# Transposing x and u by crossbar DMA transfers in place of TensorE, in a convolution followed by a token-and-channel mixing layer

## The chip, the cores and the metric

The kernel runs on one core of a Trainium2 chip. The metric is device time in microseconds (us) of one execution, median of several runs; "the granted clock" is the share of full speed that the throttle gave TensorE. PE is TensorE (matmul), PEld its weight load, DVE VectorE, ACT ScalarE, POOL GpSimd, SP SyncE; SPq, ACTq and POOLq are these engines' sequencers, which here mostly issue DMA transfers.

## The reference

```python
# x: (8, 4224, 192); batch B = 8, tokens S = 4224, channels D = 192
x = causal_conv7(x, softmax(weight))           # 8 heads, 7 taps
theta = x @ w_theta                            # 192 x 192
zr, zi = x * cos(theta), x * sin(theta)
y = einsum('ts,bsd->btd', w_tok_r, zr) + einsum('ts,bsd->btd', w_tok_i, zi)   # 4224 x 4224 twice
u = x + y
out = u + relu(u @ w_ch)                       # 192 x 192
```

The two token products are nearly all of the arithmetic. In both kernels the two channel products take their left operand with channels on the partitions. x and u are made with tokens on the partitions, so both are transposed; how that is done is what this study changes.

## The kernel before

Tokens are cut into 33 chunks of 128. A chunk is built once: convolution by TensorE (`conv`), transposition (`transpose`), `theta`, cosine and sine, products with x, and sums. It then stays in SBUF as `z` for 17 steps of token matmuls. There are 58 steps. Each handles one pair of row blocks of the token matrices and up to 11 live chunks, in 7 runs (a step of 11 chunks has 7 x 11 x 2 = 154 matmuls of 128x384). 11 chunks are built in the opening, before the steps flow freely; the other 22 are built in two later stages, about two a step. In the last 17 steps (the final ones) each step also finishes its rows: `cast` u to fp16, transpose it, `output`. The last five, with fewer live chunks, are called late.

Work is emitted in program order with positions: a task at position p of a step comes before the matmul at p/7 of it. In the traces each of PE, DVE, ACT and POOL works in that order; a scheduler places the transfers of SP's one queue.

```python
    def transposed(u, by_dve=False):
        tp = banks("tp", F16)                    # one of two PSUM buffers, shared with pc and v
        for k in range(6):
            pe(nc.tensor.transpose(
                tp[:, 0, k * P : (k + 1) * P], u[:, k * P : (k + 1) * P], ident
            ))
        uT = wk.tile([P, 6, P], F16, name="uT", tag="uT")
        evacuate(uT[:, :, :].rearrange("p k s -> p (k s)"), tp[:, 0, 0 : 6 * P], by_dve)
        return uT
# ... cut ...
        def conv(self, j):
            # ... cut: 8 matmuls into pc, evacuated by ACT into self.x ...
            if j == 1:
                for a in range(NQ):
                    t0 = token(self.k, a)
                    nc.sync.dma_start(
                        out=xs[t0 : t0 + Q, :], in_=self.x[a * Q : (a + 1) * Q, :]
                    )

        def transpose(self, g):
            self.xT[g] = transposed(
                self.x[:, g * GC : (g + 1) * GC], 0 < self.k < 3 or (self.k, g) == (0, 1)
            )

        def theta(self, g):
            v = channel_mix(self.xT[g], wth).rearrange(
                "p k (b h e) -> p k b h e", b=2, h=2
            )
            # ... cut: two ACT sines of v into z ...
# ... cut ...
        def turn_u(self, i, g):
            self.uT[i, g] = transposed(self.ub[i, g])
# ... cut: outputs(), times in us after the step's end ...
                    at = 0.7 + 12 * i
                    every, turn, mix = 3.6, 2.9, 4.7
# ... cut: step_events(t), positions of a new chunk's ten tasks (conv x2, transpose x2, theta x2, products, sums);
# the kernel after has eleven, with the store of x after the transposes ...
                pos = [0, .5, 1.3, 1.6, 2.1, 2.5, 3.1, 3.15, 3.4, 3.6]
# ... cut: the opening, one turn per chunk; old is the chunk before ...
        if ch:
            ch.conv(0)
        between(2)
        if old:
            old.theta(0)
        between(1)
        if ch:
            ch.conv(1)
        # ... cut ...
        if old:
            old.theta(1)
        # ... cut ...
        if ch:
            ch.transpose(0)
        if old:
            old.product(Z11)
        between(1)
        if ch:
            ch.transpose(1)
```

## Time and profile before

| | before |
|---|---|
| time | 1468.77 us (3 runs, 1468.66 to 1469.96) |
| PE busy | 98% of the span |
| token matmuls | 81% of the chain that ended last |
| granted clock | 0.996 |
| DMA share | 0.6 in quiet stages, 1.0 or more in the opening and the chunk stages |

From the page of the kernel before: busy us of each engine with its share of the span; the chain that ended last; groups of instructions (line, engine, operation, tiles, count, busy us, mean ns of one, idle time of the engine just before); issues of transfers, with median us to landing.

```profile
PE 1434.6 (98%) x10095; PEld 905.6 (62%) x10095; DVE 1001.0 (68%) x1050; ACT 360.7 (25%) x461; POOL 430.3 (29%) x659
...
PE 91%; DVE 3%; ACT 3%; DMA 1%; issue 1%; POOL 0%; DVEq 0%; ACTq 0%; POOLq 0%
PE y L408 81%; PE v L138 6%; PE tp L153 3%; ACT z L233 2%; PE pc L196 2%; DMA st<-in_moe_w_tok_i_dram 1%; DVE pv L373 1%; DVE z L244 1%; DVE z L238 0%; DVE wt L308 0%; DVE pv L437 0%; ACT uT L148 0%; DVE wt L320 0%; ACT pv L371 0%; ACT z L148 0%
...
L408 PE MATMUL y<-z,wt 128*128 128x384 f16 x7656 | 1295.3, 326 | 7.7 <-DVE pv L373 6.8
...
L148 ACT ACTIVATE uT<-tp 128x768 f16<-128x768 f16 x127 | 102.3, 813 | 296.8 <-PE tp L153 294.9
...
L138 PE MATMUL v<-wch,uT 128*128 128x192 f16 x528 | 56.9, 254 | 3.5 <-DVE pv L437 1.9
L138 PE MATMUL v<-wth,uT 128*128 128x192 f16 x528 | 54.3, 246 | 3.1 <-ACT z L233 3.0
...
L153 PE MATMUL tp<-ident,z 128*128 128x128 f16 x396 | 33.4, 222 | 8.8 <-ACT z L233 8.3
...
pv<-part SPq DMA_DIRECT2D x79, 768.0 KB, 5.4
out_dram<-pv SPq DMA_DIRECT2D x66, 384.0 KB, 4.5
st<-in_moe_w_tok_r_dram POOLq DMA_DIRECT2D x136, 176.0 KB, 5.8
...
xs<-z SPq DMA_DIRECT2D x132, 96.0 KB, 4.5
```

PE almost never waits: 7.7 us before the token matmuls in the whole span, 3.1 us before the theta products. The theta products wait for ACT's sines (z, L233: 3.0 of the 3.1 us), which read the PSUM buffer that the product takes, never for a transfer.

Windows of the kernel before: stretch, its length, busy us of each engine with instruction counts, granted clock, mean DMA share of the 16 engines (over 1 where packets overlap), GB/s.

```profile
50.00:100.00 50.00, 43.39 (x396) 28.27 (x394) 42.38 (x61) 42.72 (x58) 15.77 (x28) 1.00 0.98 221
500.00:600.00 100.00, 100.00 (x767) 63.64 (x765) 76.25 (x89) 38.02 (x48) 27.44 (x49) 1.00 1.04 248
1300.00:1400.00 100.00, 99.52 (x739) 66.05 (x738) 71.78 (x70) 25.51 (x33) 36.08 (x43) 1.00 0.91 212
```

In the opening (50 to 100 us) PE is 87% busy, and in the chunk stage from 500 us it is full while the DMA engines already show a share of 1.04. What a group of six transposes costs is read from starts in the timeline (start, duration, engine, line, instructions), since ends of matmuls are modelled:

```profile
1083.34 0.50 PE L153 MATMUL tp<-ident,ub 128*128 128x128 f16 x6
1083.68 1.79 PE L408 MATMUL y<-z,wt 128*128 128x384 f16 x10
1085.30 0.82 PE L138 MATMUL v<-wch,uT 128*128 128x192 f16 x8
```

The group holds PE for 1083.68 - 1083.34 = 0.34 us.

### The profile page before, as it was taken

The page shows a single profiled execution, that of the slowest core. Times are in us where ns is not written, and L with a number is a line of the kernel's source. Part 1 is how long each engine was busy: PE and PEld are TensorE (multiplying, and loading weights), DVE is VectorE, ACT ScalarE, POOL GpSimd, SP SyncE. Part 2 cuts the span into 40 slices and gives each one's busy share as a digit, 9 for nine tenths or more (in the row PEclk, how much of TensorE's full clock was granted, in tenths as well). Part 3 has the DMA queues.
Part 4 walks back from the last instruction along what each step waited for, and adds up shares of the span by engine and source line. Part 5 has one row for each costly group of instructions (what it writes and reads, how often), then busy time and mean ns, then how long its engine had stood idle before and what let it go on. Part 6 is the DMA issues. An engine that isn't in the chain of part 4 may idle for free.

```text
span 1469.8 us, 24434 instructions
## 1 busy us (share of the span) xinstructions
PE 1434.6 (98%) x10095; PEld 905.6 (62%) x10095; DVE 1001.0 (68%) x1050; ACT 360.7 (25%) x461; POOL 430.3 (29%) x659
## 2 busy tenths in 40 slices
PE   7789999999999999999999999999999999999997
PEld 4556666666666666666666666666666666666665
DVE  6884655454548687766656658769777787778575
ACT  6861101111134353000000015254122222121224
POOL 7422211111223322211113232332233333453220
PEclk9999999999999999999999999999999999999998
DMA  9976756574699999887879989999778777999873
GB/s 172 227 155 145 144 104 144 96 151 89 149 232 212 232 224 263 193 198 167 209 162 239 200 194 229 201 232 256 128 191 197 173 182 185 224 237 217 196 201 108
DMA packets 234975, 274.16 MB, mean 187 GB/s; under 512 B 69104, under 2 KB 202608, under 8 KB 234864
## 3 DMA queue, kind: packets, MB, share of 16 engines
q0 software_dynamic: 163616, 95.30, 49.0%
q1 hardware_dynamic: 71248, 177.30, 34.1%
q8 instruction: 79, 1.29, 0.3%
q14 instruction: 32, 0.26, 0.1%
HBM read 245.49 MB, written 111.28 MB: 243 GB/s over the span
## 4 chain that ended last, share of the span: by engine, by line
PE 91%; DVE 3%; ACT 3%; DMA 1%; issue 1%; POOL 0%; DVEq 0%; ACTq 0%; POOLq 0%
PE y L408 81%; PE v L138 6%; PE tp L153 3%; ACT z L233 2%; PE pc L196 2%; DMA st<-in_moe_w_tok_i_dram 1%; DVE pv L373 1%; DVE z L244 1%; DVE z L238 0%; DVE wt L308 0%; DVE pv L437 0%; ACT uT L148 0%; DVE wt L320 0%; ACT pv L371 0%; ACT z L148 0%
## 5 line engine op out<-in xcount | busy, mean ns | idle before, releaser
L408 PE MATMUL y<-z,wt 128*128 128x384 f16 x7656 | 1295.3, 326 | 7.7 <-DVE pv L373 6.8
L408 PEld LDWEIGHTS <-wt 128*128 128x128 f16 x7656 | 737.5, 98 | 475.0 <-issue 10.4
L373 DVE TENSOR_TENSOR pv<-y,pv 128x768 f32<-128x768 f32 x324 | 308.5, 953 | 374.2 <-PE y L408 348.6
L308 DVE STREAM_TRANSPOSE wt<-st 128x1408 f16<-128x1408 f16 (+7 forms) x224 | 326.4, 1463 | 7.7 <-DMA st<-in_moe_w_tok_i_dram 7.0
L295 POOL DMA_DIRECT2D st<-in_moe_w_tok_i_dram x232 | 132.7, 581 | 497.7 <-DVE wt L308 473.7
L295 POOL DMA_DIRECT2D st<-in_moe_w_tok_r_dram x232 | 132.7, 581 | 459.0 <-DVE wt L308 443.7
L320 DVE TENSOR_TENSOR wt<-wt 128x1408 f16<-128x1408 f16 (+7 forms) x216 | 204.1, 945 | 9.5 <-PE y L408 6.6
L148 ACT ACTIVATE uT<-tp 128x768 f16<-128x768 f16 x127 | 102.3, 813 | 296.8 <-PE tp L153 294.9
L148 ACT ACTIVATE z<-pc 128x768 f16<-128x768 f32 x65 | 52.9, 814 | 386.5 <-PE pc L196 386.5
L371 ACT ACTIVATE pv<-y 128x768 f32<-128x768 f32 x66 | 53.7, 813 | 281.5 <-PE y L408 281.5
L138 PEld LDWEIGHTS <-uT 128*128 128x128 f16 x1056 | 93.0, 99 | 25.9 <-issue 9.9
L437 DVE SCALAR_TENSOR_TENSOR pv<-v,pv 128x768 f32<-128x768 f32 x66 | 62.7, 949 | 46.8 <-PE v L138 45.5
L183 POOL DMA_DIRECT2D xw<-in_x_dram x132 | 76.5, 591 | 35.8 <-issue 10.1
L427 ACT ACTIVATE ub<-pv 128x768 f16<-128x768 f32 x66 | 54.8, 837 | 90.6 <-DVE pv L373 89.5
L244 DVE TENSOR_TENSOR z<-z 128x768 f16<-128x768 f16 x132 | 73.4, 556 | 3.8
L233 ACT ACTIVATE z<-v,half_pi 128x768 f16<-128x768 f32 x66 | 59.6, 903 | 40.0 <-PE v L138 39.8
L238 DVE TENSOR_TENSOR z<-z 128x1536 f16<-128x1536 f16 x66 | 60.4, 950 | 10.8 <-ACT z L233 10.8
L355 POOL TENSOR_TENSOR pv<-pv,xr 128x1536 f32<-128x1536 f32 x20 | 62.9, 3144 | 7.9 <-issue 4.5
L138 PE MATMUL v<-wch,uT 128*128 128x192 f16 x528 | 56.9, 254 | 3.5 <-DVE pv L437 1.9
L138 PE MATMUL v<-wth,uT 128*128 128x192 f16 x528 | 54.3, 246 | 3.1 <-ACT z L233 3.0
L233 ACT ACTIVATE z<-v 128x768 f16<-128x768 f32 x66 | 53.2, 805 | 0.0
L153 PE MATMUL tp<-ident,z 128*128 128x128 f16 x396 | 33.4, 222 | 8.8 <-ACT z L233 8.3
(43 smaller groups left out, 201.5 us busy)
## 6 DMA issues: line engine op xcount, KB each, us to landing
part<-pv SPq DMA_DIRECT2D x79, 768.0 KB, 4.3
pv<-part SPq DMA_DIRECT2D x79, 768.0 KB, 5.4
out_dram<-pv SPq DMA_DIRECT2D x66, 384.0 KB, 4.5
st<-in_moe_w_tok_r_dram POOLq DMA_DIRECT2D x136, 176.0 KB, 5.8
st<-in_moe_w_tok_i_dram POOLq DMA_DIRECT2D x136, 176.0 KB, 4.9
xs<-z SPq DMA_DIRECT2D x132, 96.0 KB, 4.5
xw<-in_x_dram POOLq DMA_DIRECT2D x121, 96.0 KB, 5.9
part<-xs POOLq DMA_DIRECT2D x26, 384.0 KB, 7.4
```

Of the source, the lines that this page charges most:

```text
L138: pe(nc.tensor.matmul(v[:, k, b * D : (b + 1) * D], lhsT=tT[:, 3 * k + b + i, :], rhs=w[:, 2 * b + i, :], start=(i == 0), stop=(i == 1),))
L148: act(nc.scalar.activation(out=out, in_=in_, func=AT.Copy))
L153: pe(nc.tensor.transpose(tp[:, 0, k * P : (k + 1) * P], u[:, k * P : (k + 1) * P], ident))
L183: nc.gpsimd.dma_start(out=self.xw[lo : lo + n, h, :, :], in_=x[:, t0 : t0 + n, :].rearrange("b s d -> s b d"),)
L233: act(nc.scalar.activation(**args))
L244: dve(nc.vector.tensor_tensor(out=z[:, o, :], in0=z[:, a, :], in1=z[:, b, :], op=ALU.subtract))
L295: pool(nc.gpsimd.dma_start(out=st[a * Q : (a + 1) * Q, 0:nb, :, 0:n] .rearrange("i r bt s -> i (r bt) s"), in_=w[self.tbs[0] * P : (self.t ...
L308: dve(nc.vector.transpose(self.w[name][:, 0 : self.n, :, :], self.st[int(name[1])][:, int(name[0]) - 1, :, 0 : self.n * Q] .rearrange("p b ...
L320: dve(nc.vector.tensor_tensor(out=self.w[name][:, 0 : self.n, :, :], in0=self.w[a][:, 0 : self.n, :, :], in1=self.w[b][:, 0 : self.n, :, : ...
L355: pool(nc.gpsimd.tensor_tensor(out=self.pv[i], in0=self.pv[i], in1=xr, op=ALU.add))
L373: dve(nc.vector.tensor_tensor(out=o, in0=yv, in1=o, op=ALU.add))
L408: pe(nc.tensor.matmul(y[cn][:, q, 0:BH], lhsT=self.w[wn][:, c, :, :].rearrange("p bt i -> p (bt i)"), rhs=chunks[k].z[:, zn, q * BH : (q + ...
```

## The change

The intent: take the transposes and their evacuations off TensorE, ACT and the two PSUM buffers, and let the DMA crossbar transpose directly from SBUF to SBUF. To make room and time for this, uT gets four buffers (the token weights one fewer), the transposition comes straight after the convolution, the store of x comes after it, and the uses are moved later. The late steps keep TensorE.

```diff
+    def turned():
+        return wk.tile([P, 6, P], F16, name="uT", tag="uT", bufs=4)
+
+    def crossed(u):
+
+        uT = turned()
+        nc.sync.dma_start(out=uT, in_=u, transpose=True)
+        return uT
+
     def transposed(u, by_dve=False):
# ... cut ...
-            if j == 1:
-                for a in range(NQ):
# ... cut: the store of x, now in its own method store(), called after transpose ...
         def transpose(self, g):
-            self.xT[g] = transposed(
-                self.x[:, g * GC : (g + 1) * GC], 0 < self.k < 3 or (self.k, g) == (0, 1)
-            )
+            self.xT[g] = crossed(self.x[:, g * GC : (g + 1) * GC])
# ... cut ...
-            return wpool.tile([P, NW, NQ, Q], F16, name="wt", tag="wt", bufs=11)
+            return wpool.tile([P, NW, NQ, Q], F16, name="wt", tag="wt", bufs=10)
# ... cut ...
-            self.uT[i, g] = transposed(self.ub[i, g])
+            self.uT[i, g] = (transposed if self.late else crossed)(self.ub[i, g])
# ... cut ...
-                    at = 0.7 + 12 * i
-                    every, turn, mix = 3.6, 2.9, 4.7
+                    at = (8.5 if i else 0.9 - self.time / 7) if self.pair else 0.7
+                    every, turn, mix = 3.6, 1.7, 9.0
# ... cut ...
-                pos = [0, .5, 1.3, 1.6, 2.1, 2.5, 3.1, 3.15, 3.4, 3.6]
+                pos = [0, .4, .8, .81, .82, 2.6, 3.0, 3.6, 3.65, 3.9, 4.1]
# ... cut: the opening ...
             ch.conv(1)
+        if ch:
+            for g in range(NG):
+                ch.transpose(g)
+            ch.store()
# ... cut ...
-        if ch:
-            ch.transpose(0)
         if old:
             old.product(Z11)
-        between(1)
-        if ch:
-            ch.transpose(1)
+        between(2)
```

More of the change, by code (lines that the diff above doesn't have):

```diff
@@ L155, in transposed @@
             ))
-        uT = wk.tile([P, 6, P], F16, name="uT", tag="uT")
+        uT = turned()
         evacuate(uT[:, :, :].rearrange("p k s -> p (k s)"), tp[:, 0, 0 : 6 * P], by_dve)
@@ L209, in conv, with store @@
             )
-            if j == 1:
-                for a in range(NQ):
-                    t0 = token(self.k, a)
-                    nc.sync.dma_start(
-                        out=xs[t0 : t0 + Q, :], in_=self.x[a * Q : (a + 1) * Q, :]
-                    )
+        def store(self):
+            for a in range(NQ):
+                t0 = token(self.k, a)
+                nc.sync.dma_start(
+                    out=xs[t0 : t0 + Q, :], in_=self.x[a * Q : (a + 1) * Q, :]
+                )
         def transpose(self, g):
-            self.xT[g] = transposed(
-                self.x[:, g * GC : (g + 1) * GC], 0 < self.k < 3 or (self.k, g) == (0, 1)
-            )
+            self.xT[g] = crossed(self.x[:, g * GC : (g + 1) * GC])
         def theta(self, g):
@@ L253, in tasks @@
                 yield lambda g=g: self.transpose(g)
+            yield self.store
             for g in range(NG):
```

## The prediction

> **What bounds the kernel.** TensorE. The page shows PE busy 1434.6 of 1469.8 us and 91% of the chain that ended last, 81% in the token matmuls y. From 200 to 400 us the windows show PE 100% busy: there a TensorE microsecond is a kernel microsecond. ACT (25%) and DVE (68%) are hidden. Exceptions: the first 92 us (11 chunks built in turn, about 7.9 us each at the end; PE idle about 20 us in the first 100, ACT and DVE about 85% busy from 50 to 100 us) and the last 60.
>
> **Removed.** 684 transposes (instruction order): 66 groups of six for x, 48 for u (12 full final steps); the late steps keep 18. The timeline shows the cost: token matmuls start every 0.1625 us, and from a group's first transpose (1083.34) to the next token matmul (1083.68) is 0.34 us, though the group is listed with 0.50. So 114 x 0.34 = 38.8 us of PE: 16.3 for u, 15.0 for x of the 22 later chunks, 7.5 in the opening. Some 114 evacuations of 0.81 us (ACT) or 0.56 us (DVE) go too, and one user of the two PSUM buffers.
>
> **Added.** 114 crossbar transfers of 192 KB on the SP queue; this trace has none. Other SP transfers land in 4.3 to 5.4 us; [...]. I take 5 us to landing under load for six (an estimate from these). DMA share is already 1.0 in 400-600 us. One weight buffer fewer (10), enough by my count.
>
> **What is on the path.** In the steady stages a transfer has about 6.4 us (x) and 7.3 us (u) until first use, so I expect it hidden with few waits: 31 us gained, less 2 to 5 for late landings and slower weight loads. In the opening it isn't hidden: evacuation of chunk i, transfer, theta, two sines (1.7 us), evacuation of chunk i+1 (0.8) form a loop through in-order engines: period = landing + about 3.6 us. At 5 us that is 8.6 us in place of 6.5 to 7.9; at 4 us 7.6. SP also issues eight other transfers a chunk. So the opening loses up to 15 us, or gains a few, since ACT loses 1.6 us a chunk.
>
> Sum: -31 +4 (steady), about 0 (opening, -7 to +15): **1442 us, range 1425 to 1466**. Chances: faster by over 2% (under 1439.4) 0.45; within 2% 0.49; slower 0.06.
>
> **What would show each step.**
> - PE matmul count down by 684, busy down by 30 to 40 us; ACT copies uT<-tp down to about 18.
> - Full final steps shorter by 1.36 us (4 x 0.34) of about 27.
> - Waits: PE v on DMA uT nearly all in the first 100 us, under 5 us after that.
> - Opening: PE continuously busy from 92 us before, 85 to 107 after.
> - Issues: uT landing at 4 to 6 us, 1 to 2 us of SP issue each.
>
> **What would make it wrong.** Landings over 7 us (a crossbar slower than a copy, or SP blocked by row loads that wait up to 6.5 us for a buffer): then PE waits at each theta and output mix, and the gain is gone. Crossbar traffic that delays the weight loads, seen as DVE waits at the transposes of wt. Or landings of 3 us: the opening gains 10 us, total near 1425.

## The result, and the profile after

The kernel after took 1538.58 us in the median (1523.26 to 1543.67, 4 runs), before 1469.05 us (4 runs). The ratio is 1.0455 (95% interval 1.038 to 1.053): slower. Ratios are the mean time of one kernel's fast runs over that of the other's of the same rounds, so not quite the ratio of the medians quoted here.

From the page of the kernel after, the lines that answer to those above (line numbers have moved: the token matmul is now L417, the addition of its result L382):

```profile
PE 1431.6 (93%) x9413; PEld 878.0 (57%) x9413; DVE 993.1 (64%) x1045; ACT 278.4 (18%) x352; POOL 429.2 (28%) x659
...
PE 67%; DMA 19%; DVE 7%; issue 3%; ACT 2%; POOL 2%; SPq 1%; DVEq 0%; POOLq 0%; ACTq 0%
PE y L417 61%; DMA uT<-z 10%; PE v L138 5%; DMA uT<-ub 3%; DVE pv L382 2%; DVE wt L317 2%; DMA st<-in_moe_w_tok_r_dram 2%; DMA xw<-in_x_dram 1%; DMA st<-in_moe_w_tok_i_dram 1%; DVE wt L329 1%; ACT z L241 1%; PE pc L205 1%; DVE pv L446 1%; POOL st L304 1%; DMA out_dram<-pv 1%
...
L138 PE MATMUL v<-wth,uT 128*128 128x192 f16 x528 | 66.5, 279 | 63.7 <-DMA uT<-z 62.5
...
L138 PE MATMUL v<-wch,uT 128*128 128x192 f16 x528 | 55.0, 248 | 19.8 <-DMA uT<-ub 17.4
```

The transposes are gone: 684 fewer instructions on PE would be 9411, the page has 9413 (two more of the opening's filler matmuls). But the chain now holds 19% DMA (the crossbar transfers are 13% of the span), and the channel products, which had waited 3.1 us (theta) and 3.5 us (output), wait 63.7 and 19.8 us, nearly all for transfers.

The issues of the kernel after, with median us to landing. Further below, from its uT tile, come the transfers' issue time on SP in ns (minimum, median, maximum), first and last start in us, and all transfers' us from issue to landing.

```profile
pv<-part SPq DMA_DIRECT2D x79, 768.0 KB, 6.2
out_dram<-pv SPq DMA_DIRECT2D x66, 384.0 KB, 6.2
...
xs<-z SPq DMA_DIRECT2D x132, 96.0 KB, 5.1
...
uT<-z SPq DMA_TRANSPOSE x66, 6.7
...
uT<-ub SPq DMA_TRANSPOSE x48, 6.4
```

The row loads (5.4 before), the outputs (4.5 before) and the stores of x (4.5 before) all land later too. The issue times and landings from the tile uT of the kernel after:

```profile
L156 SPq DMA_TRANSPOSE uT<-z x66: 1211/1324/3992, 11.8 to 1079.2; - x66
L156 SPq DMA_TRANSPOSE uT<-ub x48: 1209/1334/4671, 1114.2 to 1453.7; - x48
...
DMA to landing us min/median/max: 2.5/6.6/15.7
```

A landing of 6.6 us in the median, the issue time included, is about as long as the whole time that the schedule left until first use (6.4 us for x, 7.3 us for u). Whether a transfer comes late then depends on the stage. The landings of uT in the kernel after, in the chunk stage from 440 to 620 us, in the first full final steps (1100 to 1290 us) and in the later ones (1290 to 1470 us):

```profile
DMA to landing us min/median/max: 4.7/6.7/10.0
...
DMA to landing us min/median/max: 2.5/5.1/7.8
...
DMA to landing us min/median/max: 5.4/9.1/15.7
```

PE waited for uT eight times in the first of these windows (16.4 us), never in the second, nine times in the third (17.4 us). One turn in the chunk stage shows how, in the timeline of the kernel after:

```profile
502.90 5.32 SPq L430 DMA_DIRECT2D part<-pv  x2
...
507.37 7.32 PE L417 MATMUL y<-z,wt 128*128 128x384 f16 x44
...
508.44 0.32 SPq L353 DMA_DIRECT2D pv<-part  x1
508.85 4.33 SPq L156 DMA_TRANSPOSE uT<-z  x2
...
516.22 0.83 PE L138 MATMUL v<-wth,uT 128*128 128x192 f16 x8 [1.53 <-DMA uT<-z]
516.89 1.46 PE L417 MATMUL y<-z,wt 128*128 128x384 f16 x8
...
519.94 0.83 PE L138 MATMUL v<-wth,uT 128*128 128x192 f16 x8 [1.58 <-DMA uT<-z]
```

The two crossbar transfers are issued behind a 768 KB row load and two 768 KB row stores in the same queue, and PE, which executes in order, stands still for 1.53 and 1.58 us at the two theta products.

Windows of the kernel after:

```profile
50.00:100.00 50.00, 32.87 (x242) 20.13 (x240) 32.52 (x48) 27.87 (x37) 18.54 (x33) 0.84 1.25 215
500.00:600.00 100.00, 88.44 (x623) 53.20 (x621) 70.40 (x85) 27.11 (x34) 27.23 (x49) 0.98 1.09 213
1300.00:1400.00 100.00, 91.43 (x599) 57.10 (x597) 69.99 (x65) 9.79 (x12) 43.38 (x44) 0.98 1.07 222
```

PE falls from 43 to 33 busy us of 50 in the opening, from 100 to 88 in the chunk stage, from 99.5 to 91 in the second half of the final steps. Its granted clock fell too: 0.84 in place of 1.00 in this part of the opening, 0.98 in the other two windows. In this trace it is granted either full or half speed, in pieces of 3.4 us and multiples of it (3.413 to 385.7 us, but for a last piece of 2.6 us). Each of the 17 half-speed pieces between 20 and 1520 us follows a window of 3.4 us in which PE was busy, by this trace, for 0 to 48%, and of the windows of this length (on the grid of the pieces) that full speed followed, the least busy had 43%. So about 1.8 us or more of standing lay in the window before each of these half-speed pieces.

A late transfer thus cost more than its wait here. In the two chunk stages the clock was halved for 34.1 us, and token matmuls started 320 ns apart there in place of 163. PE was busy for 30.8 us of these, so the half clock cost some 15 us (an estimate: half of that busy time). This is why PE's busy time in the two stages did not fall: it rose by 4.0 us over before, though 44 groups of transposes were gone (in no_turn, below, it fell by 13.6 us). PE stood for 41.2 us there in place of 2.9, 34.1 us of it for uT.

The best map of the loss comes from the token matmuls. There are 7656 of them in every kernel in the same order, so the start of the n-th tells how far a kernel is behind. Us behind (+) or ahead (-) of before, in the profiled runs (read from the starts in the traces, good to 0.2 us; the columns end at matmuls 540, 4600, 5540, 6863 and 7655):

| kernel | end of opening | + chunk stage 2 | + chunk stage 3 | + 8.6 full final steps | end |
|---|---|---|---|---|---|
| after | +22.8 | +43.1 | +65.2 | +58.7 | +76.4 |
| no_turn | -8.0 | -13.8 | -19.3 | -27.2 | -30.7 |
| plain_copy | +12.4 | +15.5 | +16.9 | +10.1 | +6.9 |
| plain_256 | +22.2 | +32.4 | +42.0 | +34.8 | +31.8 |
| plain_split | +25.0 | +36.9 | +50.6 | +40.0 | +45.5 |
| half | +18.0 | +25.4 | +33.5 | +26.4 | +22.9 |
| act_ring | +41.9 | +74.7 | +119.2 | +112.1 | +115.4 |
| shadow | +16.7 | +32.9 | +54.4 | +54.4 | +75.1 |
| x_only | +22.3 | +44.1 | +67.6 | +67.6 | +67.7 |
| u_only | 0.0 | 0.0 | -0.4 | -7.2 | -0.9 |
| opening_pe | -0.1 | +15.2 | +31.2 | +23.9 | +37.2 |
| x_slack | 0.0 | +5.2 | +12.7 | +7.0 | +18.9 |
| x_slack_u | -0.7 | +6.6 | +17.5 | +5.7 | +16.9 |
| u_first8 | -0.2 | -0.2 | -0.6 | -6.5 | -6.4 |
| u_rows_late | -0.3 | -0.3 | -0.7 | -12.5 | -7.9 |

The kernel after loses about equally in the opening and in each chunk stage, gains 6.5 us in the first full final steps, as intended, and gives back 17.7 us at the end. The other rows are the experiments.

### The profile page after: what moved, and what is told of

It reads as the page before. It is cut to its first block, busy times and chain, and to the rows that moved or that the text cites. A ratio compares the mean times of both kernels' runs of the same rounds, so it can differ in the third digit from the quotient of the medians.

```text
span 1542.0 us, 23166 instructions
## 1 busy us (share of the span) xinstructions
PE 1431.6 (93%) x9413; PEld 878.0 (57%) x9413; DVE 993.1 (64%) x1045; ACT 278.4 (18%) x352; POOL 429.2 (28%) x659
## 4 chain that ended last, share of the span: by engine, by line
PE 67%; DMA 19%; DVE 7%; issue 3%; ACT 2%; POOL 2%; SPq 1%; DVEq 0%; POOLq 0%; ACTq 0%
PE y L417 61%; DMA uT<-z 10%; PE v L138 5%; DMA uT<-ub 3%; DVE pv L382 2%; DVE wt L317 2%; DMA st<-in_moe_w_tok_r_dram 2%; DMA xw<-in_x_dram 1%; DMA st<-in_moe_w_tok_i_dram 1%; DVE wt L329 1%; ACT z L241 1%; PE pc L205 1%; DVE pv L446 1%; POOL st L304 1%; DMA out_dram<-pv 1%
## 5 line engine op out<-in xcount | busy, mean ns | idle before, releaser
L417 PE MATMUL y<-z,wt 128*128 128x384 f16 x7656 | 1295.8, 329 | 10.1 <-DVE pv L382 8.7
L417 PEld LDWEIGHTS <-wt 128*128 128x128 f16 x7656 | 747.5, 99 | 501.3 <-issue 28.3
L382 DVE TENSOR_TENSOR pv<-y,pv 128x768 f32<-128x768 f32 x324 | 308.0, 951 | 398.0 <-PE y L417 368.4
L329 DVE TENSOR_TENSOR wt<-wt 128x1408 f16<-128x1408 f16 (+7 forms) x216 | 197.4, 914 | 22.1 <-PE y L417 18.2
L138 PEld LDWEIGHTS <-uT 128*128 128x128 f16 x1056 | 97.2, 105 | 115.2 <-DMA uT<-z 72.8
L138 PE MATMUL v<-wth,uT 128*128 128x192 f16 x528 | 66.5, 279 | 63.7 <-DMA uT<-z 62.5
L138 PE MATMUL v<-wch,uT 128*128 128x192 f16 x528 | 55.0, 248 | 19.8 <-DMA uT<-ub 17.4
L205 PE MATMUL pc<-xw,bands 96*64 96x192 f16 x528 | 39.4, 276 | 6.8 <-DMA xw<-in_x_dram 5.3
L205 PEld LDWEIGHTS <-bands 96*64 96x64 f16 x528 | 23.4, 119 | 30.2 <-issue 20.6
```

The lines of the kernel that those rows point to most:

```text
L138: pe(nc.tensor.matmul(v[:, k, b * D : (b + 1) * D], lhsT=tT[:, 3 * k + b + i, :], rhs=w[:, 2 * b + i, :], start=(i == 0), stop=(i == 1),))
L205: pe(nc.tensor.matmul(pc[half * 2 * Q : (half + 1) * 2 * Q, h // 2, h % 2 * B * G : (h % 2 + 1) * B * G], lhsT=bands[:, 4 * j + h, :, :].r ...
L329: dve(nc.vector.tensor_tensor(out=self.w[name][:, 0 : self.n, :, :], in0=self.w[a][:, 0 : self.n, :, :], in1=self.w[b][:, 0 : self.n, :, : ...
L382: dve(nc.vector.tensor_tensor(out=o, in0=yv, in1=o, op=ALU.add))
L417: pe(nc.tensor.matmul(y[cn][:, q, 0:BH], lhsT=self.w[wn][:, c, :, :].rearrange("p bt i -> p (bt i)"), rhs=chunks[k].z[:, zn, q * BH : (q + ...
```

## The experiments

Fifteen kernels ran, each timed against before on the same chip (before: 1470 to 1471 us in every group). Theories that recur: **late** (transfers land after their use, and PE stands), **crowd** (their packets slow the other transfers), **queue** (their place in SP's one queue makes them late), **crossbar** (a crossbar transfer is slower than a copy).

### no_turn: no transposition at all

Crossbar transfers left out; the products read one constant tile. Wrong result.

```diff
     def crossed(u):
-        uT = turned()
-        nc.sync.dma_start(out=uT, in_=u, transpose=True)
-        return uT
+        return still
```

> The kernel after with every crossbar transfer left out: theta and the output mix read one constant tile (wrong result on purpose). It has neither the TensorE transposes nor the transfers. If a removed group of six transposes is worth 0.34 us of TensorE, this runs near 1430 us (1469 - 38.8), perhaps 10 us less because the opening also loses its wait for a transposed x; a step without chunks gets no shorter, a full final step 1.36 us shorter. If the removed groups were worth less than I read (hidden behind weight loads), it is above 1445 us.

Measured: 1445.97 us (1441.21 to 1449.58), ratio 0.9834 (0.9814 to 0.9855). The ceiling of the change is 24 us (1470.1 - 1446.0), not 38.8, and 8 us of the profiled run's gain is the opening's freedom from any transposed x. The expectation left a gap between 1430 and 1445, and the result fell at its upper edge: the group's 0.34 us is right for PE, but not all of it reaches the end. From matmul 5540 to 6863 (8.6 steps) the kernel wins 7.9 us, 0.92 us a step in place of 1.36. The trace shows part of the rest as new PE waits for a free result buffer: 15.1 us before y on DVE pv, in place of 6.8 before. (In u_rows_late, below, where PE does not wait in these steps, they win 1.37 us each.) Since no_turn keeps all other edits of the change (ten weight buffers, the later uses), these are not what made the kernel after slower.

### shadow: TensorE transposes kept, crossbar transfers beside them, read by nobody

```diff
+    def shadow(u):
+        spare_uT = wk.tile([P, 6, P], F16, name="sT", tag="sT", bufs=2)
+        nc.sync.dma_start(out=spare_uT, in_=u, transpose=True)
+
-    def transposed(u, by_dve=False):
+    def transposed(u, by_dve=False, also=True):
+        if also:
+            shadow(u)
```

(also=False in the late steps; ten weight buffers.)

> The kernel before, TensorE transposes kept and used, and beside each of the 114 groups the same crossbar transfer into a buffer that nobody reads. Theory A (the loss is waiting for a transfer whose landing of 6.6 us in the median comes after its use): nobody waits here, so within 1% of before, 1469 to 1484 us, with landings as long as in the kernel after. Theory B (the extra 87,552 packets of 256 B take DMA time from the weight and row loads, and these stop the engines): slower by over 2%, over 1500 us, with waits at weight transposes or row loads.

Measured: 1546.68 us, ratio 1.0518 (1.0483 to 1.0552). This looked like the end of "late", but the waits show that my experiment did not isolate what I wanted. Nobody reads the result, yet a transfer also holds its source: x may not be overwritten by the sums, and the fp16 copy of u may not be rewritten, until it has been read.

The waits of the run shadow (who, for whom, us in total, times, longest):

```profile
ACT ub L433 <- DMA sT<-ub: 51.3, 15, 6.0
DVE z L250 <- DMA sT<-z: 44.0, 14, 7.0
POOL pv L361 <- DMA xr<-xs: 33.3, 9, 17.6
```

So it shows that late transfers hurt without any reader, through their sources, and that other loads (xr) come late too. It does not separate "late" from "crowd". Of what "crowd" had predicted, longer waits for weight loads are hardly there: the weight transposes wait 9.6 us for transfers, 7.7 us before.

### plain_copy: the same bytes, queue and waits, without the crossbar

```diff
-        nc.sync.dma_start(out=uT, in_=u, transpose=True)
+        nc.sync.dma_start(out=uT[:, :, :].rearrange("p k s -> p (k s)"), in_=u)
```

> The kernel after with a plain copy of the same 192 KB from SBUF to SBUF in the place of each crossbar transfer (wrong result on purpose), same queue, order and waits. If the crossbar is what makes landings long (768 packets of 256 B and about 1.3 us of issue), landings fall from 6.6 to under 4.5 us and the time to under 1470 us. If the place in the SP queue and behind the bulk transfers makes them long, landings stay over 5 us and the time over 1500 us.

Measured: 1480.05 us (1473.96 to 1482.85), ratio 1.0063 (1.004 to 1.0085); wrong result. Between the two expectations: landings were 5.4 us in the median, so a transfer in this place takes most of the landing without the crossbar, but the time fell by 58 us. A plain copy in the same place costs 34 us over no_turn; being a crossbar transfer costs 58 more. "Queue" alone is refuted as the whole cause.

### act_ring: the transfers issued by ACT

```diff
-        nc.sync.dma_start(out=uT, in_=u, transpose=True)
+        act(nc.scalar.dma_start(out=uT, in_=u, transpose=True))
```

> The kernel after with all crossbar transfers issued by ACT, in place of SP; nothing else changed, result right. Theory A1 (transfers are late because they stand in SP's one queue: behind row loads that wait for a buffer, and in the ring behind 768 KB row transfers): landings fall to about 3 to 4 us, TensorE's waits for uT fall from 80 to under 25 us, and the time to under 1480 us. Theory A2 (the 16 DMA engines are shared, whatever the queue): landings stay over 6 us and the time over 1510 us.

Measured: 1591.39 us in the median of four, one of them slow; 1576.90 to 1600.22 us in the three fast runs, whose ratio is 1.0793 (1.0726 to 1.0859). Landings are 7.3 us in the median, and PE waits 107.7 us for uT in place of 79.9. Issued by ACT the transfers did not land sooner (7.3 us in place of 6.6). Landings and time are as theory A2 expected; that shared DMA engines are the cause is not shown. In addition ACT, which computes sines in order, now spends 1.4 us (median) issuing each transfer of x.

### plain_256: the plain copy in packets of 256 B

The packet records of the traces gave the next theory. A crossbar transfer of 192 KB is 768 packets of 256 B (87,552 in the kernel after, over 114 transfers), the plain copy 128 of 1536 B. While weights are being loaded (packets of mostly 704 B in POOL's queue), the two queues start about as many packets each. Counts of packets started per us in the kernel after, own tabulation of the records:

```
us      POOL-queue packets    crossbar packets
1359    205                   203
1360    200                   202
1361    213                   189
1362    209                   199
```

At 200 packets per us, 768 packets need 3.8 us. Over all 114 transfers, from the first to the last packet: 1.4 us in the mean where under 20 packets of POOL's queue fell into it (47 transfers), 4.2 us where over 500 did (24). The counts are nearly one to one (205 and 203, 200 and 202, 213 and 189, 209 and 199 per us); that the two queues take turns packet by packet is my inference from them.

```diff
-        nc.sync.dma_start(out=uT[:, :, :].rearrange("p k s -> p (k s)"), in_=u)
+        nc.sync.dma_start(out=uT[:, :, 0:P], in_=u.rearrange("p (k s) -> p k s", s=P))
```

(uT rows padded to P + 8, so that each 256 B is a packet of its own.)

> The plain copy of the run before, cut into 768 packets of 256 B each, as a crossbar transfer has, in place of 128 of 1536 B: the destination rows are padded (wrong result on purpose). Theory P (the cost is the number of packets: in the packet records of the kernel after, the SP ring and the weight-load ring take turns packet by packet, about 200 each per us, so 768 packets need some 3.8 us while weights are loading): landings go back from 5.4 to over 6 us and the time from 1480 to over 1510 us. Theory X (the crossbar itself, its issue of 1.3 us or its transposing write, is the cost): within 1% of the plain copy, 1470 to 1495 us.

Measured: 1499.67 us (1494.35 to 1510.05), ratio 1.0204 (1.0163 to 1.0246), median landing 5.7 us. Cutting the same bytes into 768 packets costs 20 of the 58 us (the issue is 0.1 us longer, too: 0.60 to 0.66 us in the median, 0.47 to 0.55 in plain_copy). Both theories were half right: neither 1510 nor 1495 was reached.

### half: crossbar transfers of three blocks in place of six

```diff
-        nc.sync.dma_start(out=uT, in_=u, transpose=True)
+        nc.sync.dma_start(out=uT[:, 0:3, :], in_=u[:, 0 : 3 * P], transpose=True)
```

(the product reads blocks 0 to 2 twice; wrong result.)

> The kernel after with crossbar transfers of three blocks in place of six (384 packets of 256 B; the product reads blocks 0 to 2 twice, wrong result on purpose). Theory P: landings fall from 6.6 to about 5 us and at least half of the 58 us between the kernel after and the plain copy go: under 1510 us. Theory X with a fixed cost for each transfer (start of a crossbar transfer, not its packets): over 1520 us.

Measured: 1491.68 us, ratio 1.0143 (1.0126 to 1.016), median landing 5.2 us. Half the packets take 47 us off, though each transfer still takes 1.2 us of issue. The cost grew here with the amount sent through the crossbar; it was not mainly a fixed cost of each transfer.

### plain_split: the 256 B copy issued in two halves

```diff
-        nc.sync.dma_start(out=uT[:, :, 0:P], in_=u.rearrange("p (k s) -> p k s", s=P))
+        for h in range(2):
+            nc.sync.dma_start(
+                out=uT[:, 3 * h : 3 * h + 3, 0:P],
+                in_=u[:, 3 * h * P : (3 * h + 3) * P].rearrange("p (k s) -> p k s", s=P),
+            )
```

> The plain copy in 256 B packets (1500 us), issued as two transfers of half the data each, so that SP spends about 1.3 us on a group, as on a crossbar transfer, with the same packets (wrong result on purpose). It tells apart what the crossbar costs beyond its packets, 38 us. Theory I (SP's longer issue): the time rises to 1525 us or more. Theory S (stalls of the crossbar: in the packet records of the kernel after, 702 packets of 256 B took over 0.5 us, of the plain copy none): it stays under 1510 us.

Measured: 1511.46 us (1509.63 to 1514.2), ratio 1.0278 (1.0265 to 1.0291). The longer issue costs 12 us (this pair of halves also has a second completion to wait for, so 12 us is an upper value for the issue itself). 27 us between this run and the kernel after are left, and the spread of the kernel after alone makes this uncertain by 11 us. What distinguishes the records is stalls: in the kernel after 702 crossbar packets took over 500 ns, and the packets over 100 ns add up to 0.6 us for each transfer on each of the 16 engines; in plain_256 no packet of 256 B took even 100 ns (three in this run, at most 201 ns). But the stalls hardly lengthen a transfer itself: from its first to its last packet it takes 2.28 us in the mean in the kernel after, 2.02 us in plain_256.

### quiet: crossbar transfers and 256 B copies side by side in quiet steps

The kernel before with 48 extra transfers, six a step, a step of crossbar transfers and a step of 256 B copies by turns, between 150 and 355 us. Their sources are weight tiles just made.

```diff
+    def extra(t, name):
+        src = steps[t + 1].w[name][:, 0:6, :, :].rearrange("p c b i -> p (c b i)")
+        if t % 2:
+            sT = wk.tile([P, 6, P], F16, name="sT", tag="sT", bufs=1)
+            nc.sync.dma_start(out=sT, in_=src, transpose=True)
+        else:
+            sP = wk.tile([P, 6, P + 8], F16, name="sP", tag="sP", bufs=1)
+            nc.sync.dma_start(
+                out=sP[:, :, 0:P], in_=src.rearrange("p (k s) -> p k s", s=P)
+            )
```

> The kernel before with 48 extra transfers of 192 KB, read by nobody, in eight quiet steps of 25 us (about 150 to 350 us, DMA share 0.6): six a step, some 3 us apart, by turns a step of crossbar transfers and a step of plain copies in 768 packets of 256 B (result right). If the stalls belong to crossbar transfers as such, packets of over 0.1 us appear in the crossbar steps and none in the plain steps, and crossbar landings are longer, about 4 to 5 us beside 3 to 4. If they come only from the crowd in the busy stages, there are none here. The time stays within 1% of before, under 1484 us, since nobody waits.

Measured: 1477.11 us, ratio 1.0042 (1.0023 to 1.006), result right. The tile of the crossbar transfers of the run quiet, issue time and landing:

```profile
L474 SPq DMA_TRANSPOSE sT<-wt x24: 1211/1214/2189, 182.9 to 353.0; - x24
...
DMA to landing us min/median/max: 2.7/4.4/8.9
```

The tile of its copies in 256 B packets:

```profile
L477 SPq DMA_DIRECT2D sP<-wt x24: 593/595/866, 156.8 to 329.9; - x24
...
DMA to landing us min/median/max: 2.6/4.4/9.4
```

Landings are alike (my expectation of longer ones was wrong), and so are the packets where nothing else moves: 1.08 us from first to last packet by the crossbar, 0.98 us by the copy. But packets over 100 ns appear in 13 of the 24 crossbar transfers (together 0.04 to 1.4 us on each engine), and in one of the 24 copies (two packets, 0.02 us). So in this run the stalls belong to the crossbar, and they come when other traffic is about: none of the ten crossbar transfers beside which no other packet ran has one. Of the 6 us that the kernel takes longer, the profiled run has 4.6 us in one place, after a weight sum waited 10.7 us until an extra crossbar transfer had read its source; weight sums wait for copies too (21.9 us in all), without loss. That the stalls are the remaining 27 us of plain_split is not shown: no run could take the stalls alone away, and they lengthen a transfer by little. What the profiled runs do show of this remainder (31 us at the last token matmul): PE stands 103.0 us in the kernel after and 82.3 us in plain_split, and the half clock costs some 12 us more (estimated as above).

### x_only and u_only: one part of the change each

x_only: `turn_u` and the times of casts and outputs as before. u_only: x as before; u as after.

```diff
# x_only, against after
-            self.uT[i, g] = (transposed if self.late else crossed)(self.ub[i, g])
+            self.uT[i, g] = transposed(self.ub[i, g])
# u_only, against before
-            self.uT[i, g] = transposed(self.ub[i, g])
+            self.uT[i, g] = (transposed if self.late else crossed)(self.ub[i, g])
```

> Crossbar for x alone, u by TensorE with the old times (result right). In the kernel after the token matmuls had fallen behind by 22.8 us in the opening and by 42.4 us in the two later stages that build chunks. If each part costs by itself: 1525 to 1540 us.

> Crossbar for u of the full final steps alone, x by TensorE as before (result right). In the kernel after, the first seven full final steps won 7.5 us over before and the rest lost 18.7 us. If the loss comes from the transfers in the queue (row loads and stores before and behind them), it comes back: 1475 to 1485 us. If it was the aftermath of delays from earlier stages, all twelve steps win about 1.1 us: 1453 to 1460 us.

Measured: x_only 1531.24 us, ratio 1.0413 (1.0395 to 1.0431); u_only 1463.45 us (1462.08 to 1466.85), ratio 0.9953 (0.9938 to 0.9968). Nearly all of the loss is x's. u by itself gains half a percent; the time lies between what I had expected of either cause. In its profiled run it is 7.9 us ahead by 1307 us and has lost this by 1365 us.

### opening_pe: the opening's chunks by TensorE, the rest as after

```diff
-            self.xT[g] = crossed(self.x[:, g * GC : (g + 1) * GC])
+            if self.k < NW:
+                self.xT[g] = transposed(
+                    self.x[:, g * GC : (g + 1) * GC], 0 < self.k < 3 or (self.k, g) == (0, 1)
+                )
+            else:
+                self.xT[g] = crossed(self.x[:, g * GC : (g + 1) * GC])
```

(with the two calls of `transpose` back in their old places of the opening.)

> The kernel after with the 11 chunks of the opening transposed by TensorE as before, the rest by crossbar (result right). In the kernel after the token matmuls were 22.8 us behind before's at the end of the opening. If that loss is the opening's own: 1510 to 1520 us, with PE continuously busy from about 92 us again. If it only comes back later: above 1530 us.

Measured: 1507.06 us, ratio 1.0247 (1.0234 to 1.026). The opening's loss vanishes (-0.1 us at its end) and 31 us come back, somewhat more than the 22.8 us seen there.

### x_slack: 2.5 us more between the transfer of x and its use

On top of opening_pe:

```diff
-                pos = [0, .4, .8, .81, .82, 2.6, 3.0, 3.6, 3.65, 3.9, 4.1]
+                pos = [0, .4, .8, .81, .82, 3.3, 3.7, 4.1, 4.15, 4.4, 4.6]
```

> The run with the opening by TensorE (1507 us), with theta and all that follows it 0.5 to 0.7 of a run later in the chunk stages, which gives each transfer of x some 2.5 us more before its use (result right). Theory A (TensorE waits because a transfer lands after its use): waits of TensorE for uT<-z fall from 28 to under 8 us, and 15 us or more of the 26 us that the chunk stages lose there come back: 1482 to 1494 us. If the shared DMA engines slow everything, whatever the use: over 1500 us.

Measured: 1486.87 us (1480.86 to 1499.24), ratio 1.0121 (1.0064 to 1.0179). The wait of theta for x in opening_pe (us in total, times, longest):

```profile
PE v L138 <- DMA uT<-z: 27.7, 17, 4.1
```

The same wait in x_slack:

```profile
PE v L138 <- DMA uT<-z: 14.7, 9, 4.8
```

PE's waits are halved, not as far as expected (under 8 us). The two chunk stages lose 12.7 us in place of 31.2 us, and 20 us of the time come back. The half-clock time of the two stages falls with the waits, from 23.9 to 3.4 us. The transfers of x did not get faster (landings 7.4 and 7.3 us in the median in the two stages, 6.8 and 6.4 in opening_pe); only their use came later. This is the direct demonstration of "late": the schedule's slack, not the DMA load as such, decided 18.5 of the 31.2 us lost in the chunk stages.

### u_first8 and u_rows_late: two attempts to keep u's gain

u_first8 uses the crossbar in the first eight full final steps only. u_rows_late issues a step's row loads after its last two crossbar transfers:

```diff
# u_first8, against u_only
+            self.cross = not self.late and 0 <= t + NU - NSTEP < 8
-            self.uT[i, g] = (transposed if self.late else crossed)(self.ub[i, g])
+            self.uT[i, g] = (crossed if self.cross else transposed)(self.ub[i, g])
# u_rows_late, against u_only (row loads and crossbar transfers also kept in this order on SP)
-            found.append((1.6, steps[t + 1].load_rows))
+            found.append((4.0 if steps[t].final and not steps[t + 1].late else 1.6,
+                          steps[t + 1].load_rows))
-                    found.append((3.3 + 1.7 * i, lambda i=i: steps[t + 1].add_x(i)))
+                    found.append(((4.1 if steps[t].final else 3.3) + 1.7 * i,
+                                  lambda i=i: steps[t + 1].add_x(i)))
```

> Crossbar for u of the first eight full final steps alone, the last four and all x by TensorE (result right). In the profile of the run with u alone the token matmuls got 7.9 us ahead of before's over the first ten of these steps and then lost 8 us. So this should end at 1460 to 1464 us, with PE waits for uT under 2 us. If the loss is not in the transfers of the last steps but in the other times of casts and outputs, the gain goes here too: 1468 us or more.

> The run with u alone, with the row loads of the next step issued after the step's last two crossbar transfers in place of before them (and the additions of x after that), so that no transfer stands in SP's queue behind a row load that waits for the landing of an output (result right). Theory Q (the last steps lose because transfers stand behind such row loads): TensorE's waits for uT in the last four full steps vanish, all twelve steps win 0.7 us: 1459 to 1462 us. If the late row loads or the shared DMA engines are the cause, it is no better than the run with u alone: 1463 us or more, with waits for pv or uT.

Measured in five rounds: u_first8 1462.34 us (1461.47 to 1462.62), ratio 0.9943 (0.993 to 0.9956); u_rows_late 1461.70 us (1458.98 to 1466.99), ratio 0.9944 (0.9927 to 0.9961). u_first8 does what was expected: 6.5 us ahead, kept to the end, and no wait of PE for uT. u_rows_late is 12.5 us ahead by matmul 6863 and then loses 4.6 us with 7.2 us of PE waits for uT<-ub in three places: the order of the queue was part of the late steps' loss, not all. From matmul 5540 to 6863 its PE does not wait at all (3.7 us in u_only), and it wins 11.8 us, 1.37 us a step; before waited for 0.2 us there, so this is the removed work itself. Both results are right; they are the fastest right kernels, by 0.6%, and not distinguishable from each other.

### x_slack_u: everything that helped x and u together

x_slack with the row loads of u_rows_late.

> The run before this, with the order of the row loads of the run u_rows_late in the final steps as well, which had gained 9 us there over before (result right): the version with all that helped. If both effects add: x_slack less about 20 us, so 1462 to 1474 us; it can beat the run with u alone (1463 us) only if x by crossbar now gains something in the chunk stages, where leaving the transposes out gained 11 us.

Measured: 1484.96 us (1477.13 to 1487.67), ratio 1.0085 (1.0056 to 1.0114). The effects did not add: no better than x_slack within its spread. In its profiled run the chunk stages still lose 18 us. x by crossbar does not pay in any version tried.

## Why the prediction was wrong

Predicted: 1442 us, 1425 to 1466. Measured: 1538.58 us. The direction was wrong. Point by point:

- **What bounds the kernel** was right: PE, with every microsecond of it counting. That cuts both ways: PE, working in order, waited 79.9 us for uT in the kernel after, whose token matmuls ended 76.4 us behind.
- **Removed, "114 x 0.34 = 38.8 us"**: right for a group where PE has nothing else to wait for, too large as a sum. A full final step won the predicted 1.36 us in u_rows_late (1.37), where PE did not wait in these steps; it won 0.92 us in no_turn and 0.76 us in the kernel after (6.5 us over 8.6 steps), where new waits before y, on DVE pv, took 2.8 and 3.3 us. With nothing put in the place of the transposes the whole kernel won 24 us (no_turn).
- **"I take 5 us to landing under load"**: measured 6.6 us in the median, 2.5 to 15.7, its issue of 1.3 us included; the second of two transfers also stands behind the issue of the first. I reasoned from medians of other transfers, which have larger packets (768 to 6144 B); a crossbar transfer's 768 small packets took 4.2 us in the mean where over 500 weight packets fell among them, 1.4 us where under 20 did.
- **"In the steady stages a transfer has about 6.4 us (x) and 7.3 us (u) until first use, so I expect it hidden with few waits: 31 us gained"**: this is the step that failed. In the chunk stages, where landings were 6.7 and 6.8 us in the median, PE waited at 15 of the 44 transfers, 2.3 us each in the mean, and its clock was halved for 34.1 us. The two stages lost 42.4 us (65.2 - 22.8) in place of gaining 15.0; only the first full final steps, with landings of 5.1 us, gained. I compared one typical number with one slack, though the same profile showed the DMA share at 1.04 in that stage, where the landings then spread from 4.7 to 10.0 us (440 to 620 us). x_slack shows it: 2.5 us more slack, same landings, 20 us back.
- **"In the opening it isn't hidden ... period = landing + about 3.6 us", "-7 to +15"**: the loop was right, the size too small. The first transfers of chunks 2 to 10 start at 29.0 and 114.1 us, 10.6 us apart in the mean, where TensorE's transposes started 8.0 us apart (25.8 and 89.9 us). Two terms of the sum were too small: the 22 landings were 5.9 us in the mean, not 5, and the issue of the first of a chunk's two transfers, 1.3 us, was left out (5.9 + 1.3 + 3.6 = 10.8 us, an estimate from these). Loss 22.8 us; opening_pe brings it back.
- **"PE v on DMA uT ... under 5 us after that"**: in the kernel after it waits 62.5 us for x and 17.4 us for u, 28.3 us of this in the first 160 us. PE's busy time, expected to fall by 30 to 40 us, fell by 3.0 us (1434.6 to 1431.6), for the half clock above (some 15 us in the two chunk stages alone, the estimate given there).
- **"What would make it wrong"** named landings over 7 us and the gain gone, and said nothing of a loss of this size. It gave this a chance of 0.06.

Where the 67 us went, as steps from one kernel to the next (ratios times 1470 us; from the intervals of the ratios the steps are good to 3 to 7 us, the last to 11 us):

| from | to | what was added | us |
|---|---|---|---|
| before | no_turn | transposes left out | -24 |
| no_turn | plain_copy | 192 KB transfers in SP's queue, used on landing | +34 |
| plain_copy | plain_256 | 768 packets in place of 128 (and 0.1 us more issue) | +21 |
| plain_256 | plain_split | issue twice as long (and two completions) | +11 |
| plain_split | after | the crossbar itself; stalled packets seen, not isolated | +26 |

Each step holds both PE's waits and the half clock that came with them. Open: the cause of that last step; and what else than the order of the queue delays the transfers of the last full final steps, where u_rows_late still lost 4.6 us.

## What to carry to other kernels

Before moving work from a full TensorE to a transfer, compare the slack with the slow transfers of that stage, not with a median landing: TensorE, working in program order, stood at 15 of the 44 transfers of the chunk stages, 2.3 us each in the mean, and paid again with a halved clock (34.1 us). Count packets as well as bytes, since 768 packets in place of 128 for the same bytes cost 21 us here; and try the move stage by stage, since one part of a change (here u in the first final steps, -0.6%) may pay while the whole loses 4.7% or so. A plain copy in the same place, cut to the same packets, is a cheap way to tell what the special transfer costs.
